# Attention loads issued one step ahead, two buffers for a head's keys and queries, attention steps dealt over fewer slices

## The chip, the cores and the metric

The kernel runs on one core of one Trainium2 chip. The metric is the device time of one execution in microseconds (us); the figure for a kernel is the median of its runs. PE is TensorE, DVE VectorE, ACT ScalarE, POOL GpSimd; SP is SyncE, whose queue issues the DMAs spoken of here.

## What is computed

The reference, cut to what matters. The inputs are q, k, v of shape (4, 8, 576, 64), a memory M_prev with its normaliser z_prev, beta, and the weights of two feed-forward layers with 512 model columns and 1536 hidden columns.

```python
# attention, per batch b and head h (S = 576, D = 64)
scores = where(causal, -1e9, q @ k.T / sqrt(D)); a = softmax(scores)
local = a @ v
q_p = where(q > 0, q, exp(q) - 1) + 1
mem_out = (q_p @ M_prev) / (q_p @ z_prev + 1e-6)
out = g * mem_out + (1 - g) * local              # g = sigmoid(beta)
# tokens: (4 * 576) x 512, heads side by side
# layer 0
xn = x / rms(x) * rms_g
x = (silu(xn @ w_gate) * (xn @ w_val)) @ w_out
# layer 1
x = (sigmoid(x @ w_gate2) * (x @ w_val2)) @ w_out2
```

## The kernel before

The 2304 tokens are worked in five groups: group -1 holds the first 128 tokens of all four batches (512 columns), groups 0 to 3 the other 448 tokens of one batch each. For a group, both feed-forward layers run in 12 slices of 128 hidden columns: a slice loads its weights (`weights`, `slot`), makes the gate and value products (L961), the gate (`gated`: tanh on ACT at L981, products on DVE at L983, L986 and L990, the two halves of h at L998/L999 or L1005/L1006) and, one slice later, 12 output products (`out_share`, L1027). In the trace group -1 stands from about 45 to 266 us, group 0 to 464, group 1 to 664, group 2 to 852, group 3 to 1009.

While PE works on group g, the attention of group g+1 is made beside it. It is cut into steps, put in a row by `att_steps`: for each head u `att_qk` (loads keys kd and queries qd, two DMAs each into the two halves of the partitions, casts them on ACT and takes the remainder on DVE, L210 to L231), `att_scores` (scores on PE at L253, copied to SBUF by ACT at L550, maxima, softmax), `att_av`, after every second head `att_mem` (loads ph, exp(q) at L629, L630, L631, products with the memory at L638) and `att_measure` (loads qm for the group after, sums of absolute values at L188); once per group `att_vmax` and `att_vsplit` (L150 to L174: values in two f16 parts).

The steps are dealt between the slices by the main loop (L1437 to L1522). `DUE` says how many slices before the end of a group the last step is dealt, `HOLD` how many slices pass before the first, and `AFTER` behind which slice's gate (counted back) a step's instructions may be issued; each is indexed by g+1. A scheduler then sets the order of every engine's queue, and each engine works its queue in that order. SP's queue holds the loads of the attention and those of the weights. A tile with `bufs=1` has a single buffer, so its next load waits until the last reader of the one before is done.

## Time and profile before

| | |
|---|---|
| median of 3 runs | 1013.91 us (1009.89 to 1014.56) |
| the profiled execution, its own time | 1016.42 us |
| its span | 1014.6 us, mean granted clock of PE 0.996 |
| PE busy | 999.3 us (98%) |
| DVE, ACT, POOL busy | 832.1 (82%), 654.7 (65%), 201.8 us (20%) |
| DMA | 243.74 MB, 240 GB/s on average |

The profile is of one execution. Busy time of PE counts matmuls, at whichever clock they ran. An idle time in brackets behind a row of the timeline is that of its engine just before the instruction, with what ended it; xN says that N instructions of one form stand in one row.

### The profile page before, as it was taken

Reading aid. Unit: us, or ns where it says so; the run is one execution under the profiler, and the core shown is the slowest. Engines: PE = TensorE matmul, PEld = TensorE weight load, DVE = VectorE, ACT = ScalarE, POOL = GpSimd, SP = SyncE. Lnnn points to the kernel's source line nnn. Section 1 sums busy time; section 2 is a strip of 40 time slices with the busy share of each in tenths; the row PEclk is TensorE's granted clock in tenths of the full one; section 3 lists DMA queues with packets and bytes.
Section 4 is the critical chain, followed back from the end, with each engine's and each line's share of the span. In section 5 each row is a group of like instructions: output and inputs, shape, how many; then the busy total and the mean of one; then the engine's idle time right before and its main releaser. Section 6 shows DMA issues by size and latency. Waiting matters only on the chain.

```text
span 1014.6 us, 19021 instructions
## 1 busy us (share of the span) xinstructions
PE 999.3 (98%) x6721; PEld 700.0 (69%) x6721; DVE 832.1 (82%) x1826; ACT 654.7 (65%) x1238; POOL 201.8 (20%) x339
## 2 busy tenths in 40 slices
PE   9999999999999999999999999999999999999998
PEld 6878887888666676666666765555567556876885
DVE  6989999997769998775998977757779776995883
ACT  7668887786678888674778676535456353543452
POOL 4203221141004233300424432002133100000000
PEclk9999999999999999999999999999999999999999
DMA  9599998986894676498779856995544256836521
GB/s 350 180 373 398 345 352 257 376 308 200 272 368 172 224 251 229 177 322 240 246 257 322 266 179 224 309 340 167 174 144 167 83 159 212 284 135 226 201 84 37
DMA packets 102561, 243.74 MB, mean 240 GB/s; under 512 B 25154, under 2 KB 37058, under 8 KB 102466
## 3 DMA queue, kind: packets, MB, share of 16 engines
q1 hardware_dynamic: 102322, 242.41, 69.8%
q8 instruction: 53, 0.87, 0.3%
q14 instruction: 42, 0.34, 0.1%
q10 hardware_dynamic: 144, 0.11, 0.0%
HBM read 187.43 MB, written 51.38 MB: 235 GB/s over the span
## 4 chain that ended last, share of the span: by engine, by line
PE 65%; DVE 14%; issue 9%; DMA 6%; ACT 5%; POOL 1%; SPq 0%; DVEq 0%; POOLq 0%; ACTq 0%
PE po L1027 20%; PE pg L961 16%; PE pv L961 15%; PE pw L1137 7%; PE ps L253 2%; DMA qd<-in_qT 1%; PE pm L638 1%; POOL sc L555 1%; DVE mx L572 1%; DMA raw<-in_w 1%; DMA wr<-kept 1%; PE pav L589 1%; PE pav L591 1%; PE pav L590 1%; DVE w L878 1%
## 5 line engine op out<-in xcount | busy, mean ns | idle before, releaser
L555 POOL TENSOR_SCALAR_AFFINE_SELECT sc<-sc 128x128 f32<-128x128 f32 (+1 forms) x128 | 73.0, 583 | 194.1 <-ACT sc L550 193.3
L1027 PE MATMUL po<-h,ws 128*128 128x448 f16 (+2 forms) x468 | 107.6, 375 | 0.0
L961 PEld LDWEIGHTS <-ws 128*128 128x128 f16 x552 | 53.5, 99 | 53.1 <-issue 4.9
L1027 PE MATMUL po<-h,wl 128*128 128x448 f16 (+2 forms) x372 | 86.8, 376 | 0.1
L961 PEld LDWEIGHTS <-wr 128*128 128x128 f16 x552 | 52.8, 98 | 49.2 <-issue 3.5
L1027 PE MATMUL po<-h,wr 128*128 128x448 f16 (+1 forms) x384 | 84.9, 364 | 0.2 <-ACT h L1005 0.2
L574 POOL PARTITION_ALL_REDUCE mb<-mx x32 | 61.3, 1915 | 70.9 <-DVE mx L572 62.1
L981 ACT ACTIVATE t<-pg,unit 128x448 f32<-128x448 f32 x70 | 43.8, 626 | 40.3 <-PE pg L961 40.1
L550 ACT COPY sc<-ps 128x512 f32<-128x512 f32 (+1 forms) x96 | 52.7, 562 | 18.6 <-PE ps L253 18.5
L1027 PEld LDWEIGHTS po<-h,ws 128*128 128x128 f32 x300 | 55.9, 188 | 9.4
L961 PEld LDWEIGHTS <-wl 128*128 128x128 f16 x360 | 34.7, 98 | 31.7 <-issue 1.3
L253 PE MATMUL ps<-qq,kk 128*128 128x64 f16 (+2 forms) x280 | 53.2, 295 | 0.0
L237 ACT ACTIVATE sc<-sc,qs 128x1472 f32<-128x1472 f32 x24 | 36.6, 1526 | 23.4 <-DVE sc L580 15.4
L990 DVE SCALAR_TENSOR_TENSOR t<-t,pv 128x448 f32<-128x448 f32 (+1 forms) x52 | 32.7, 629 | 18.6 <-PE pv L961 18.3
L1027 PEld LDWEIGHTS po<-h,wl 128*128 128x128 f32 x228 | 42.5, 188 | 8.0 <-ACT h L998 0.5
L1027 PE MATMUL po<-h,wrl 128*128 128x448 f16 (+1 forms) x192 | 44.0, 374 | 1.6 <-ACT h L1005 1.4
L983 DVE SCALAR_TENSOR_TENSOR t<-t,pg 128x448 f32<-128x448 f32 (+2 forms) x50 | 30.9, 618 | 15.4 <-ACT t L981 15.3
L872 ACT ACTIVATE top<-raw 128x512 f16<-128x512 bf16 x50 | 38.0, 784 | 5.6 <-DMA raw<-in_w 4.4
L998 ACT CAST h<-t 128x448 fp32r<-128x448 f32 (+1 forms) x46 | 27.0, 586 | 19.6 <-DVE t L986 14.4
L572 DVE TENSOR_TENSOR mx<-mx,sc 128x320 f32<-128x320 f32 (+2 forms) x96 | 34.5, 359 | 4.0 <-POOL sc L555 3.1
L1155 ACT COPY sn<-pw 128x224 f32<-128x224 f32 x54 | 18.2, 341 | 30.0 <-PE pw L1137 27.9
L878 DVE SCALAR_TENSOR_TENSOR w<-raw,top 128x512 int32<-128x512 int32 x48 | 35.3, 747 | 0.8 <-ACT top L872 0.6
(437 smaller groups left out, 2870.0 us busy)
## 6 DMA issues: line engine op xcount, KB each, us to landing
raw<-in_w SPq DMA_DIRECT2D x50, 511.8 KB, 6.4
kept<-w SPq DMA_DIRECT2D x48, 256.0 KB, 5.2
ws<-parts SPq DMA_DIRECT2D x24, 512.0 KB, 5.4
wr<-half SPq DMA_DIRECT2D x23, 512.0 KB, 4.1
rawl<-in_w SPq DMA_DIRECT2D x22, 511.8 KB, 6.5
wr<-parts SPq DMA_DIRECT2D x21, 512.0 KB, 5.6
ws<-half SPq DMA_DIRECT2D x21, 512.0 KB, 4.7
kd<-in_kT SPq DMA_DIRECT2D x64, 144.0 KB, 3.5
```

What stands on the lines that cost most here:

```text
L237: nc.scalar.activation(out=sc, in_=sc, func=AF.Exp, scale=both)
L253: nc.tensor.matmul(ps[:, c0:c0 + n], kk[:, k0:k0 + 128], r[:, q0 - 128:q0 - 128 + n], start=(i == 0), stop=(i == 1))
L550: nc.scalar.copy(out=sc[:, o:o + c], in_=ps[:, 0:c])
L555: nc.gpsimd.affine_select(out=d, in_=d, compare_op=ALU.is_ge, fill=NEG, base=SQ[kt] - T0[kt], pattern=[[1, n]], channel_multiplier=-1,)
L572: nc.vector.tensor_tensor(out=mx[:, q:448], in0=mx[:, q:448], in1=sc[:, d:d + 448 - q], op=ALU.max)
L574: nc.gpsimd.partition_all_reduce(mb[:, 0:448], mx[:, 0:448], channels=128, reduce_op=bass_isa.ReduceOp.max)
L872: nc.scalar.activation(out=top.bitcast(F16).rearrange("p (n t) -> p n t", t=2)[:, :, 1], in_=raw.bitcast(BF16)[:, :, 2], func=AF.Copy)
L878: nc.vector.scalar_tensor_tensor(out=dst.bitcast(I32), in0=raw.rearrange("p n t -> p (n t)").bitcast(I32).rearrange("p (n t) -> p n t", t= ...
L961: nc.tensor.matmul(ps[:, 0:n], w[:, a, k * 128:(k + 1) * 128], x[b][:, k, o:o + n], start=(i == 0), stop=(i == 3 * KD - 1))
L981: nc.scalar.activation(out=t, in_=pg[:, 0:n], func=AF.Tanh, scale=u[:, 0:1] if half else 0.5)
L1027: nc.tensor.matmul(po[d][:, 0:n], w[2][:, a, c], hh[:, b, 0:n], start=(first and i == 0), stop=(last and i == 2))
L1137: nc.tensor.matmul(regions[m][at], left(i, m, a, k), right(j, b, k), start=first and c == 0, stop=c == 5, skip_group_check=True,)
```

## The change

- `att_load` is new: it loads keys and queries of a head. kd and qd have two buffers each, and `att_qk` of head u issues the load of head u+1 (head 0 loads both).
- `mem_load` is new: ph of a pair of heads is loaded in an `att_av`, a step ahead of `att_mem`. `measure_load` is new: qm is loaded in `att_mem`, a step ahead of `att_measure`.
- The product with the memory goes into the tile of exp(q), where it had a tile mt of its own. qd, q2 and ph are 448 columns wide; tri stands in the ring w of the weights; the tiles sn of the last group follow kd's and qd's two buffers.
- `DUE` of group 0 goes from 6 to 8: the steps that make group 1's attention are dealt over 14 slices and no longer 16. `AFTER` of group 0 goes from 1 to 2.

```diff
@@ -36,10 +36,10 @@
 NSHARE = (2, 1)
 
 ONE = (1, 12)
-DUE = (3, 6, 6, 5, 8)
+DUE = (3, 8, 6, 5, 8)
 HOLD = (1, 2, 1, 1, 1)
 BACK = (3, 3)
-AFTER = (3, 1, 3, 3)
+AFTER = (3, 2, 3, 3)
 
 HALVED = 1
 
@@ -95,7 +95,7 @@
 
     ident = const.tile([128, 128], F32, name="ident")
     make_identity(nc, ident)
-    tri = const.tile([128, 128], F32, name="tri")
+    tri = wp.tile([128, 512], F32, tag="w", bufs=4, name="tri")[:, 0:128]
     nc.gpsimd.memset(tri, 0.0)
     nc.gpsimd.affine_select(
         out=tri, in_=tri, compare_op=ALU.is_ge, fill=NEG, base=0, pattern=[[1, 128]], channel_multiplier=-1
@@ -127,7 +127,7 @@
 
     q2_ring = []
     for i in range(2):
-        t = const.tile([128, S], F32R, name=f"q2_{i}")
+        t = const.tile([128, S - 128], F32R, name=f"q2_{i}")
         nc.vector.memset(t[64:128].bitcast(F32), 0.0)
         q2_ring.append(t)
     vh1 = const.tile([128, 5, H, 65], F16, name="vh1")
@@ -178,13 +178,18 @@
 
     qring = [0]
 
+    def measure_load(g, u):
+        st["qm", g, u] = []
+        for src, c0 in ((kT, 0), (qT, 128)):
+            t = ap_.tile([128, S], F32, tag="qm", bufs=2, name="qm")[:, c0:S]
+            nc.sync.dma_start(out=t, in_=src[g, 2 * u:2 * u + 2, :, c0:S].rearrange("h d s -> (h d) s"))
+            st["qm", g, u].append(t)
+
     def att_measure(g, u):
 
         if u == 0:
             st["sums", g] = ap_.tile([128, NP, 2], F32, tag="qsum", bufs=1, name="qsum")
-        for i, (src, c0) in enumerate(((kT, 0), (qT, 128))):
-            t = ap_.tile([128, S], F32, tag="qm", bufs=2, name="qm")[:, c0:S]
-            nc.sync.dma_start(out=t, in_=src[g, 2 * u:2 * u + 2, :, c0:S].rearrange("h d s -> (h d) s"))
+        for i, t in enumerate(st.pop(("qm", g, u))):
             nc.scalar.activation(out=t, in_=t, func=AF.Abs, accum_out=st["sums", g][:, u, i:i + 1])
 
     def att_units(g):
@@ -202,18 +207,25 @@
         )
         st["qs", g] = qs
 
-    def att_qk(g, u):
-        kd = ap_.tile([128, S], F32, tag="kd", bufs=1, name="kd")
-        qd = ap_.tile([128, S], F32, tag="qd", bufs=1, name="qd")[:, 128:S]
+    def att_load(g, u):
+        kd = ap_.tile([128, S], F32, tag="kd", bufs=2, name="kd")
+        qd = ap_.tile([128, S - 128], F32, tag="qd", bufs=2, name="qd")
         for src, dst, c0 in ((kT, kd, 0), (qT, qd, 128)):
             for j in range(2):
                 nc.sync.dma_start(out=dst[64 * j:64 * j + 64], in_=src[g, u, :, c0:S])
+        st["load", g, u] = kd, qd
+
+    def att_qk(g, u):
+        if u == 0:
+            att_load(g, u)
+        if u + 1 < H:
+            att_load(g, u + 1)
+        kd, qd = st.pop(("load", g, u))
         if g < HALVED:
             q2 = q2_ring[qring[0] % 2]
             qring[0] += 1
             kk = ap_.tile([128, S], F32R, tag="kk", bufs=2, name="kk")
             qq = ap_.tile([128, S], F32R, tag="qq", bufs=2, name="qq")[:, 128:S]
-            q2 = q2[:, 128:S]
             nc.scalar.activation(out=kk, in_=kd, func=AF.Copy)
             nc.scalar.activation(out=qq, in_=qd, func=AF.Copy)
             for out, d, hi, r in ((kk, kd, kk, slice(64, 128)), (q2, qd, qq, slice(0, 64))):
@@ -601,6 +613,8 @@
         nc.vector.tensor_tensor(out=out, in0=ps[:, :, 0:64], in1=r.to_broadcast([128, n, 64]), op=ALU.mult)
 
     def att_av(g, h):
+        if h % 2 == (0 if g >= HALVED else 1):
+            mem_load(g, h // 2)
         pt = st.pop(("pt", g, h))
         s = st[g]
         ps = late["ps"].tile([128, 4, 65], F32, tag="pa", name="pav")
@@ -619,13 +633,18 @@
         nc.vector.reciprocal(out=r, in_=r)
         nc.vector.tensor_tensor(out=out, in0=ps[:, :, :, 0:64], in1=r.to_broadcast([128, 2, 2, 64]), op=ALU.mult)
 
+    def mem_load(g, u):
+        ph = st["ph", g, u] = ap_.tile([128, S - 128], F32, tag="ph", bufs=1, name="ph")
+        nc.sync.dma_start(out=ph, in_=qT[g, 2 * u:2 * u + 2, :, 128:S].rearrange("h d s -> (h d) s"))
+
     def att_mem(g, u):
 
         x = st[g]["x"]
         n = 448
-        ph = ap_.tile([128, 512], F32, tag="ph", bufs=1, name="ph")
+        ph = st.pop(("ph", g, u))
+        if HALVED <= g + 1 < B:
+            measure_load(g + 1, u)
         e = ap_.tile([128, 512], F32, tag="xn", bufs=2, name="phe")
-        nc.sync.dma_start(out=ph[:, 0:n], in_=qT[g, 2 * u:2 * u + 2, :, 128:S].rearrange("h d s -> (h d) s"))
         nc.scalar.activation(out=e[:, 0:n], in_=ph[:, 0:n], func=AF.Exp)
         nc.vector.tensor_scalar(out=e[:, 0:n], in0=e[:, 0:n], scalar1=1.0, scalar2=None, op0=ALU.min)
         nc.vector.scalar_tensor_tensor(
@@ -643,7 +662,7 @@
                     stop=True,
                 )
             gt = igate[:, None, 2 * u:2 * u + 2, None].to_broadcast([128, 2, 2, 1])
-            m = ap_.tile([128, 2, 2, 64], F32, tag="mt", bufs=2, name="mt")
+            m = e[:, 256 * i:256 * i + 256].rearrange("p (t h d) -> p t h d", t=2, h=2)
             mem_out(ps, gt, m)
             xs = x[:, 2 * i:2 * i + 2, u * 128:(u + 1) * 128]
             nc.vector.tensor_tensor(out=xs, in0=xs, in1=m.rearrange("p t h d -> p t (h d)"), op=ALU.add)
@@ -1147,7 +1166,7 @@
         cs = []
         for m, tag in ((0, "kk"), (1, "qq")):
             cs.append([ap_.tile([128, S], F32, tag=tag, bufs=2, name="cw")[:, 0:2 * n] for _ in range(2)])
-        one = [ap_.tile([128, S], F32, tag=t, bufs=1, name="sn") for t in ("kd", "qd")]
+        one = [ap_.tile([128, w], F32, tag=t, bufs=2, name="sn") for t, w in (("kd", S), ("qd", S - 128))]
         three = [ap_.tile([128, 512], F32, tag=t, bufs=1, name="sn") for t in ("mx", "mb")]
         snaps = [[one[m][:, 0:n], one[m][:, n:2 * n], three[m][:, 0:n]] for m in range(2)]
 
```

The instructions of an engine are the same in number; lines of the changed program stand up to 19 further down (L981 is L1000, L629 is L648, L1027 is L1046). Three places of the order follow. In the names, t and h are the tiles of the gate, pg and po the sums of the gate and output products, ws, wl, wr, wrl weights, x the values.

First ACT near the end of group 1's steps in group 0 (425 us in the trace). Before:

```order
L1005 ACTIVATE h<-t,unit_124 128x448
L246 CAST pt<-sc 128x1472
L830 ACTIVATE ws,sums<-ws 128x512 x2
L629 ACTIVATE phe<-ph 128x448
L550 COPY sc<-ps_5353 128x448
L981 ACTIVATE t<-pg,unit_124 128x448
L550 COPY sc<-ps_5360 128x512
L1005 ACTIVATE h<-t,unit_124 128x448
```

and with the change:

```order
L1024 ACTIVATE h<-t,unit_124 128x448
L849 ACTIVATE ws,sums<-ws 128x512 x2
L562 COPY sc<-ps_5193 128x512
L1000 ACTIVATE t<-pg,unit_124 128x448
L865 COPY unit_123<-inv 128x2
L866 ACTIVATE unit_124<-inv 128x2
L855 ACTIVATE ws<-ws,s_5837 128x512 x2
L648 ACTIVATE phe<-ph 128x448
L562 COPY sc<-ps_5203 128x448
L1024 ACTIVATE h<-t,unit_124 128x448
```

The exponential (phe) stood ahead of the gate's L981; it now stands behind the gate's L1000, two copies of units and two weight scalings. A copy of scores (sc) has moved behind the sums of ws.

Second DVE in the first heads of group 1 (300 to 306 us in the trace), from one slice's h to the next slice's t. Before:

```order
L999 TENSOR_TENSOR h<-t,h 128x448
L150 TENSOR_REDUCE am_3797<-x 128x1 x5
L715 TENSOR_SCALAR pw<-wtop 128x2
L230 SCALAR_TENSOR_TENSOR kk<-kd,qs,kk 64x576
L230 SCALAR_TENSOR_TENSOR qq<-qd,qs,qq 64x448
L153 TENSOR_REDUCE am<-am_3797 128x1
L569 TENSOR_TENSOR mx<-sc 128x448
L717 TENSOR_SCALAR inv<-pw 128x2
L983 SCALAR_TENSOR_TENSOR t<-t,pg 128x448
```

and with the change:

```order
L1018 TENSOR_TENSOR h<-t,h 128x448
L856 SCALAR_TENSOR_TENSOR ws<-wrl,s_3976,ws 128x512 x2
L734 TENSOR_SCALAR pw<-wtop 128x2
L736 TENSOR_SCALAR inv<-pw 128x2
L740 RECIPROCAL s_4153<-inv 128x2
L174 SCALAR_TENSOR_TENSOR vl<-x,sv,vh_119 128x512 x2
L581 TENSOR_TENSOR mx<-sc 128x448
L174 SCALAR_TENSOR_TENSOR vl<-x,sv,vh_119 128x512 x3
L1002 SCALAR_TENSOR_TENSOR t<-t,pg 128x448
```

The five residuals of the values (vl) stood behind this t and now stand ahead of it; the five maxima (am) and a head's kk and qq that stood here are dealt with elsewhere, the maxima further up.

Third PE in group -1 (147 to 151 us in the trace), scores of one head among the output products. Before:

```order
L1027 MATMUL po<-h,wl 128x512 x4
L253 MATMUL ps_1798<-qq,kk 128x448
L253 MATMUL ps_1798<-q_0_115,kk 128x448
L1027 MATMUL po<-h,wl 128x512 x8
L253 MATMUL ps_1805<-qq,kk 128x320
L253 MATMUL ps_1805<-q_0_115,kk 128x320
L253 MATMUL ps_1805<-qq,kk 128x192
L253 MATMUL ps_1805<-q_0_115,kk 128x192
L961 MATMUL pg<-xc,wl 128x512
```

and with the change:

```order
L1046 MATMUL po<-h,wl 128x512 x4
L265 MATMUL ps_1802<-qq,kk 128x448
L265 MATMUL ps_1802<-q_0_115,kk 128x448
L265 MATMUL ps_1809<-qq,kk 128x320
L265 MATMUL ps_1809<-q_0_115,kk 128x320
L265 MATMUL ps_1809<-qq,kk 128x192
L265 MATMUL ps_1809<-q_0_115,kk 128x192
L1046 MATMUL po<-h,wl 128x512 x8
L980 MATMUL pg<-xc,wl 128x512
```

The second part of the scores stood behind eight of the output products and now stands ahead of them.

## Rows read from the trace of the kernel before

**Rows 1.** The page, parts 1 and 2: busy time of the engines, PE's granted clock.

```profile
PE 999.3 (98%) x6721; PEld 700.0 (69%) x6721; DVE 832.1 (82%) x1826; ACT 654.7 (65%) x1238; POOL 201.8 (20%) x339
...
PEclk9999999999999999999999999999999999999999
```

**Rows 2.** Waits of PE: engine, line, released by; us in total, times, longest us.

```profile
PE pg L961 <- DMA ws<-half: 1.8, 1, 1.8
PE pg L961 <- DVE t L983: 1.6, 3, 0.7
PE po L1027 <- ACT h L1005: 1.6, 2, 1.4
```

**Rows 3.** Stretches (start:end, length; busy of PE, PEld, DVE, ACT, POOL, PEclk, DMA share, GB/s).

```profile
150.00:190.00 40.00, 39.31 (x211) 31.37 (x211) 39.63 (x75) 33.10 (x55) 5.50 (x8) 1.00 0.87 292
300.00:340.00 40.00, 39.28 (x270) 24.86 (x269) 39.11 (x85) 35.06 (x73) 13.87 (x26) 1.00 0.57 194
```

**Rows 4.** The two 10 us stretches with PE's long waits, same columns.

```profile
420.00:430.00 10.00, 8.36 (x69) 6.55 (x67) 7.49 (x26) 6.89 (x17) 4.26 (x8) 0.85 0.02 6
580.00:590.00 10.00, 7.94 (x33) 4.01 (x32) 6.66 (x21) 8.21 (x16) 5.14 (x7) 0.83 0.43 141
```

**Rows 5.** Timeline at 425 us on ACT, DVE, PE; last, 12 matmuls elsewhere (start, us, engine, instruction).

```profile
420.49 0.58 ACT L629 ACTIVATE phe<-ph 128x448 f32<-128x448 f32 x1 [0.58 <-DMA ph<-in_qT]
420.98 0.52 ACT L550 COPY sc<-ps 128x448 f32<-128x448 f32 x1
...
424.81 0.67 ACT L1005 ACTIVATE h<-t,unit 128x448 fp32r<-128x448 f32 x1 [2.31 <-DVE t L990]
...
421.10 0.39 DVE L630 TENSOR_SCALAR phe<-phe 128x448 f32<-128x448 f32 x1 [2.06 <-ACT phe L629]
...
424.16 0.62 DVE L990 SCALAR_TENSOR_TENSOR t<-t,pv 128x448 f32<-128x448 f32 x1
...
425.53 0.67 PE L1027 MATMUL po<-h,wrl 128*128 128x448 f32 x2 [1.37 <-ACT h L1005]
426.48 3.71 PE L1027 MATMUL po<-h,wrl 128*128 128x448 f32 x10 [0.28 <-DVE h L1006]
...
563.74 2.68 PE L1027 MATMUL po<-h,wl 128*128 128x448 f32 x12
```

**Rows 6.** Timeline at 583 us: SP's issue, PE.

```profile
578.47 0.58 SPq L903 DMA_DIRECT2D ws<-half  x1
...
583.43 4.13 PE L961 MATMUL pg<-hb,ws 128*128 128x448 f16 x12 [1.84 <-DMA ws<-half]
```

**Rows 7.** Waits of SP: line, released by; us in total, times, longest us.

```profile
SPq L210 <- DVE kk L230: 33.6, 15, 5.0
```

**Rows 8.** Groups of ACT: busy us, mean ns of one, idle us just before.

```profile
L227 ACT ACTIVATE kk<-kd,qs 128x576 f16<-128x576 f32 x24 | 18.6, 773 | 0.0
...
L629 ACT ACTIVATE phe<-ph 128x448 f32<-128x448 f32 x16 | 9.2, 574 | 3.2 <-DMA ph<-in_qT 3.2
...
L217 ACT ACTIVATE kk<-kd 128x576 fp32r<-128x576 f32 x8 | 5.5, 684 | 1.7 <-DMA kd<-in_kT 1.7
```

**Rows 9.** Timeline at 305 to 320 us: PE, then DVE.

```profile
309.09 2.43 PE L961 MATMUL pg<-ha,ws 128*128 128x448 f16 x12
...
317.75 2.43 PE L961 MATMUL pg<-ha,ws 128*128 128x448 f16 x12 [0.69 <-DVE t L983]
...
305.64 0.61 DVE L983 SCALAR_TENSOR_TENSOR t<-t,pg 128x448 f32<-128x448 f32 x1
306.17 0.14 DVE L158 TENSOR_SCALAR ex<-amx 128x1 int32<-128x1 int32 x1
...
312.57 2.71 DVE L174 SCALAR_TENSOR_TENSOR vl<-x,sv,vh 128x512 f16<-128x512 f32 x4
```

**Rows 10.** Timeline at 150 us: PE, then ACT.

```profile
148.45 2.02 PE L1027 MATMUL po<-h,wl 128*128 128x512 f32 x8
...
148.84 0.52 ACT L550 COPY sc<-ps 128x448 f32<-128x448 f32 x1
```

## The prediction

> **What bounds the kernel now.** I read the page first. TensorE (PE) is busy 999.3 us of a span of 1014.6, VectorE (DVE) 82%, ScalarE (ACT) 65%; PE's granted clock is at nine tenths of full or more in every slice [rows 1]. So PE bounds the kernel, and all that a new order can win is PE's idle time, 1014.6 - 999.3 = 15.3 us, and what a low clock costs. Second, PE's list of waits: the longest single ones are 1.8 us for a load of ws and 1.4 us for ACT's h; three for DVE's t hold 1.6 us in all, 0.7 at most [rows 2]. Third, the stretches: DVE is the engine to watch, at 39.63 of 40 us in group -1 and at 39.11 of 40 early in group 0, where PE misses 0.72 us [rows 3]; the two 10 us stretches with PE's long waits show a granted clock of 0.85 and 0.83, between the full and the half level [rows 4]. Last, the timelines at these two places:
>
> - Stall A, 425 us: the output product L1027 waits 1.37 us for ACT's h; its 12 matmuls, among them 0.28 us more of waiting, then take from 425.53 to 426.48 + 3.71 = 430.19, 4.66 us, against 2.68 us for 12 of the same form at 563.74 [rows 5]. Price: 1.37 + 4.66 - 2.68 = 3.35, some 3.4 us.
> - Stall B, 583 us: the gate product waits 1.84 us for ws, and its 12 matmuls take 4.13 us against 2.43 for 12 at 309 us [rows 6, 9]. Price: 1.84 + 1.70 = 3.5 us.
>
> **The change part by part.**
>
> *Keys and queries in two buffers, loaded a head ahead.* No DMA is added. Only an engine that waited for these loads can gain: ACT idled 0.0 us ahead of the 24 casts L227 and 1.7 us ahead of the 8 copies L217 (the first group's attention) [rows 8], and PE's longest waits have none on kd or qd [rows 2]. What hides the loads is work that ACT has queued ahead of the casts. SP issues all loads in order, and waits 33.6 us in 15 places for DVE's subtraction L230 before it can load kd or qd [rows 7]. The change does not take that away: the load of head u+1 is issued at step u, into the buffer of head u-1, whose last reader is the subtraction of head u-1, the same that SP waited for. The second buffer gives data one step earlier, but frees nothing queued behind kd on SP. At stall B that is the load of ws, issued at 578.47 [rows 6], and SP's order there is the same in the change. I take 0 us; bounds -1.7 (all of L217's idle) and +1.84 (one more weight load as late as ws at 583 us, because kd or qd stands ahead of it).
>
> The Trainium skill says under "DMA: Bandwidth & Descriptors", Rules for kernel authors, that a DMA should be issued early and waited for late. By that rule this part would win ACT's waits on kd, and the sum would be up to 1.7 us lower. The same page, section "Anatomy of one DMA — SWDGE (gpsimd) path", says that a semaphore wait happens on the issuing sequencer before dispatch, which speaks against the part; the trace agrees, with 33.6 us on SP, and by it the sum stays.
>
> *ph loaded ahead of its step, qm likewise.* ACT idled 3.2 us in all ahead of the 16 exponentials L629 [rows 8]. One of these reaches PE, and it is stall A: ACT came free at 420.49 - 0.58 = 419.91 and waited 0.58 us for ph, with a copy and the gate's L981 queued behind it. DVE waited 2.06 us for that exponential and then ran L630, L631 and maxima ahead of L990, from 421.10 to 424.16, 3.06 us; ACT's h followed at 424.81 and PE at 425.53 [rows 5]. The first excerpt shows the exponential behind the gate's activation, so the gate is earlier by 420.98 - 419.91 = 1.07 us. On DVE, L990 stands ahead of L630 in the change, so the 3.06 us leave the chain too, less two products of weights that come ahead instead (some 1.4 us by L174, 2.71 for four of the same width [rows 9]). 1.07 + 3.06 - 1.4 = 2.7 us is more than the 1.37 us that PE waited. I take all of stall A, -3.4 us. Bounds: -3.4, and 0, since ACT's sums of ws, which wait for their own load, still stand ahead of the gate, and h may be late again. qm: loaded a step before use, and no long wait of PE is behind it [rows 2]: 0 us.
>
> *mt dropped, tri in the ring w, q2 of 448 columns, sn in two buffers.* The same instructions on other tiles. The product with the memory makes e live longer, but e has two buffers and its exponential runs 16 times in 1014 us; tri is read before the slices begin: 0 us.
>
> *Steps of group 1 dealt over 14 of group 0's slices instead of 16, and issued one slice sooner.* The work is the same; it comes earlier, when DVE is full. The second excerpt shows the sharpest place of group 0: the five residuals L174 (2.71 us for four, 3.4 for five) and, further up, the scale's five small steps L158 to L165 (some 0.14 each, 0.7) now stand ahead of the gate's t (L983), 4.1 us more work before it. That t ended at 305.64 + 0.61 = 306.25, and PE's next gate product, which needs the bank that t frees, started at 309.09: 2.84 us of slack [rows 9]. That makes a new wait of 4.1 - 2.84 = 1.3 us. Against it, the wait of 0.69 us at 317.75 goes [rows 9], since the residuals that stood ahead of it are done. In group -1 the third excerpt has the second part of a head's scores ahead of eight output products. These began at 148.45, so the scores are now wanted then; the bank that they need is freed by ACT's copy, which ended at 148.84 + 0.52 = 149.36 [rows 10], and ACT has one more cast of a query ahead of it (some 0.5 us, by the copy of the same width): a new wait of 149.36 - 148.45 + 0.5 = 1.4 us. Both are upper ends, since a wait delays PE and so eases the next. I take half of each, +0.7 and +0.7. Bounds: 0, and the full waits with a half clock behind each, below. Groups 1 and 2 keep their order on PE, ACT, DVE and POOL, 0 us. The slices from 430 us on that lose their steps gain nothing: PE had no long wait there.
>
> **Sum.** -3.4 (A) - 0.7 (317 us) + 0.7 + 0.7 - 0.4 (one of the two other waits on DVE's t, (1.6 - 0.7)/2 [rows 2]) = -3.1. The profiled execution took 1016.42 us (span 1014.6), 2.5 above the median of the runs shown; 1016.42 - 3.1 = 1013.3, and, by the same 2.5, 1010.8 for a median. I say **1011 us**.
>
> **Rivals.**
>
> - *Faster: both drops of the clock go.* If the steps and loads that come sooner let SP reach ws at 583 us by 1.84 us earlier, stall B goes with A and the waits on DVE's t: -3.4 - 3.5 - 1.6 = -8.5, 1013.9 - 8.5 = 1005.4. For it: a shift of under 2 us is enough, and SP waits for DVE there. Against it: SP's order and DVE's order in group 1 are the same as before. Chance 0.17.
> - *Slower: the work dealt earlier makes DVE late.* Place: the gate's t at 306 us and the scores at 148 us. Price: 1.3 and 1.4 us waited, and behind each a stretch at half clock like those behind the waits of 1.37 and 1.84, worth 2.0 and 1.7 [rows 5, 6, 9]: 6.4 in all. It decides from the point where a new wait is as long as 1.37 us; behind the 0.69 at 317.75 the next 12 matmuls took 2.43, no loss [rows 9]. With stall A gone, 1013.9 + 6.4 - 3.4 = 1016.9; with stall A only moved, 1020.3. DVE at 39.11 and 39.63 of 40 us [rows 3] speaks for it; that each wait lets DVE catch up speaks against. Chance 0.18.
> - *No effect.* The loads were hidden, SP waits for the same subtraction, and stall A comes back as another late h. 1014 us. Chance 0.20.
>
> **How the numbers follow.** The forecast has the other 0.45, from 1007 to 1014. A measurement of this kernel tells about 0.5% (5 us) from no change: its three runs lie from 1009.9 to 1014.6. Faster by over that, below 1008.8: the faster rival's 0.17 and 0.11 of the forecast's, 0.28. Slower, over 1019: 0.12 of the slower rival and 0.03 of the case of no effect, 0.15. The rest, 0.57, is within it. The range runs from 1004, just under the faster rival, to 1019, between the slower one's two values; some 0.07 is left out below and 0.13 above.
>
> **What would show it.** Right: no wait of PE on ACT's h near 420 us and a clock of 1.00 there; the drop near 583 us still there, with PE on ws; SP's wait for DVE's subtraction still some 30 us; a wait of PE on DVE's t near 305 to 310 us. Wrong: the second drop gone, or a new one near 150 or 310 us; SP's wait for the subtraction halved, which would mean that the second buffer does free the queue; or a stage other than groups -1 and 0 that changed its length by over 2 us.

## The result and the profile after

The changed kernel took 1018.67 us (median of 6 runs, 1018.26 to 1022.8) against 1013.6 us of the kernel before in the same series: ratio 1.0064, 95% interval 1.0047 to 1.0081. In a second series it was 1019.03 against 1014.53 us, 1.0051 (1.0031 to 1.0071). So it is slower by 0.5 to 0.6%, some 5 to 6 us. The forecast was 1011 us and faster; the range (1004 to 1019) holds the result, the direction was wrong. In the later series the kernel before had medians from 1012.65 to 1014.53 us.

The page of the changed kernel's profile (span 1019.7 us), which answers to [rows 1]:

```profile
PE 998.2 (98%) x6721; PEld 698.0 (68%) x6721; DVE 831.1 (82%) x1826; ACT 656.1 (64%) x1238; POOL 204.9 (20%) x339
...
PEclk9999999999999999999999999999999999999999
```

PE is busy 998.2 us, 1.1 less than before, in a span 5.1 us longer. The whole loss is idle time of PE. Its list of waits (engine, line, what it waited for; us in total, times, longest) answers to [rows 2]:

```profile
PE pg L980 <- DVE t L1002: 4.3, 3, 3.2
PE pg L980 <- DMA ws<-half: 2.0, 1, 2.0
PE pg L980 <- DMA ha<-x: 2.0, 2, 1.3
PE ps L265 <- ACT sc L562: 1.4, 2, 0.8
...
PE pv L980 <- DVE t L1007: 1.1, 1, 1.1
```

Stall A, 1.4 us for ACT's h [rows 2], is gone. Stall B (ws) stands as before. New are 3.2 us in one wait for DVE's t L1002 (before: 0.7 at most), 1.3 for ha, which holds the tokens of group 1, 1.1 for DVE's t L1007, and 0.8 for the scores' copy. Two stretches of the same profile (columns as in [rows 3]), the first one answering to [rows 4]:

```profile
420.00:430.00 10.00, 10.00 (x58) 6.49 (x57) 8.45 (x18) 8.91 (x21) 1.81 (x5) 1.00 0.70 246
310.00:320.00 10.00, 6.24 (x26) 2.69 (x25) 9.63 (x17) 9.77 (x21) 3.64 (x8) 0.83 0.54 189
```

At 420 us, where before had lost 1.64 of 10 us at a granted clock of 0.85, PE is full at 1.00. Instead the stretch at 310 us, where before had no long wait [rows 9], loses 3.76 us at 0.83.

One profile is one execution, so I took three of before's order (the one shown, a repeat, and before_eph, a kernel with the same order) and three of the change's (the one shown, a repeat, and own_step_phqm, a kernel with the same order). PE's idle time by stretch, which is the length of the stretch less the time PE was busy in it, us:

| from, to (us) | before's order | change's order | mean difference |
|---|---|---|---|
| 0, 45 | 3.3, 3.7, 3.3 | 3.3, 3.3, 3.9 | +0.1 |
| 45, 262 (group -1) | 0.7, 0.7, 0.7 | 2.8, 3.1, 2.9 | +2.3 |
| 262, 300 | 0.6, 0.6, 0.6 | 0.7, 0.8, 0.7 | +0.1 |
| 300, 345 | 0.7, 0.9, 0.9 | 3.8, 3.2, 1.9 | +2.1 |
| 345, 400 | 0.4, 0.5, 0.4 | 0.8, 0.5, 1.9 | +0.7 |
| 400, 460 (stall A) | 1.6, 0.3, 1.5 | 0.0, 0.1, 0.0 | -1.1 |
| 460, 478 (tokens of group 1) | 0.0, 0.0, 0.0 | 1.3, 1.4, 1.7 | +1.5 |
| 478, 600 (stall B in it) | 3.0, 3.3, 3.2 | 3.4, 3.9, 2.4 | +0.1 |
| 600, end | 5.0, 5.0, 5.1 | 5.3, 5.4, 5.4 | +0.3 |
| idle in all | 15.3, 14.9, 15.7 | 21.5, 21.7, 20.7 | +6.0 |
| PE busy | 999.3, 994.4, 995.7 | 998.2, 995.7, 995.3 | -0.1 |
| span | 1014.6, 1009.3, 1011.4 | 1019.7, 1017.4, 1016.0 | +5.9 |

The idle time accounts for the whole difference of the spans, 5.9 us, and that is about the measured 5 to 6. The rest of the document asks what makes the new waits in group -1, at 310 us and at 464 to 477 us.

### The profile page after: what moved, and what is told of

The parts are those of the page before. It is cut to its first block, busy times and chain, and to the rows that moved or that the text cites. A ratio compares the mean times of both kernels' runs of the same rounds, so it can differ in the third digit from the quotient of the medians.

```text
span 1019.7 us, 18970 instructions
## 1 busy us (share of the span) xinstructions
PE 998.2 (98%) x6721; PEld 698.0 (68%) x6721; DVE 831.1 (82%) x1826; ACT 656.1 (64%) x1238; POOL 204.9 (20%) x339
## 4 chain that ended last, share of the span: by engine, by line
PE 75%; DMA 11%; DVE 8%; ACT 3%; issue 1%; POOL 1%; SPq 1%; ACTq 0%; POOLq 0%; DVEq 0%
PE po L1046 22%; PE pg L980 20%; PE pv L980 19%; PE pw L1156 7%; PE ps L265 3%; DMA kept<-w 2%; DMA raw<-in_w 2%; PE pm L657 1%; DMA ws<-kept 1%; PE pav L601 1%; PE pav L603 1%; PE pav L602 1%; DMA kd<-in_kT 1%; DMA rawl<-in_w 1%; DMA qk<-in_qk 1%
## 5 line engine op out<-in xcount | busy, mean ns | idle before, releaser
L1046 PE MATMUL po<-h,ws 128*128 128x448 f16 (+2 forms) x468 | 108.3, 376 | 0.3 <-ACT h L1017 0.3
L567 POOL TENSOR_SCALAR_AFFINE_SELECT sc<-sc 128x128 f32<-128x128 f32 (+1 forms) x128 | 68.8, 551 | 190.6 <-ACT sc L562 189.4
L980 PEld LDWEIGHTS <-ws 128*128 128x128 f16 x552 | 53.5, 99 | 57.6 <-issue 10.6
L1046 PE MATMUL po<-h,wl 128*128 128x448 f16 (+2 forms) x372 | 87.7, 376 | 0.3
L1046 PE MATMUL po<-h,wr 128*128 128x448 f16 (+1 forms) x384 | 86.2, 366 | 0.1
L586 POOL PARTITION_ALL_REDUCE mb<-mx x32 | 65.1, 2033 | 54.4 <-DVE mx L584 45.8
L1000 ACT ACTIVATE t<-pg,unit 128x448 f32<-128x448 f32 x70 | 43.9, 627 | 45.9 <-PE pg L980 45.6
L1046 PEld LDWEIGHTS po<-h,ws 128*128 128x128 f32 x300 | 55.6, 188 | 9.9 <-ACT h L1017 0.7
L1046 PEld LDWEIGHTS po<-h,wl 128*128 128x128 f32 x228 | 42.1, 188 | 8.1 <-DVE hb L1231 0.9
L1002 DVE SCALAR_TENSOR_TENSOR t<-t,pg 128x448 f32<-128x448 f32 (+2 forms) x50 | 30.9, 617 | 18.5 <-ACT t L1000 18.2
L1046 PE MATMUL po<-h,wrl 128*128 128x448 f16 (+1 forms) x192 | 43.4, 367 | 0.0
L587 DVE TENSOR_TENSOR sc<-sc,mb 128x896 f32<-128x896 f32 x32 | 34.8, 1087 | 3.8 <-POOL mb L586 3.8
```

What stands on the lines that cost most here:

```text
L567: nc.gpsimd.affine_select(out=d, in_=d, compare_op=ALU.is_ge, fill=NEG, base=SQ[kt] - T0[kt], pattern=[[1, n]], channel_multiplier=-1,)
L586: nc.gpsimd.partition_all_reduce(mb[:, 0:448], mx[:, 0:448], channels=128, reduce_op=bass_isa.ReduceOp.max)
L587: nc.vector.tensor_tensor(out=two, in0=two, in1=mb[:, None, 0:448].to_broadcast([128, 2, 448]), op=ALU.subtract)
L980: nc.tensor.matmul(ps[:, 0:n], w[:, a, k * 128:(k + 1) * 128], x[b][:, k, o:o + n], start=(i == 0), stop=(i == 3 * KD - 1))
L1000: nc.scalar.activation(out=t, in_=pg[:, 0:n], func=AF.Tanh, scale=u[:, 0:1] if half else 0.5)
L1046: nc.tensor.matmul(po[d][:, 0:n], w[2][:, a, c], hh[:, b, 0:n], start=(first and i == 0), stop=(last and i == 2))
```

## The experiments

### One part at a time

Four kernels on one chip; before 1012.71 us there. The theory was that the dealing alone costs, the rival that the loads do.

*loads_only*: the change with the dealing of before.

```diff
-DUE = (3, 8, 6, 5, 8)
-AFTER = (3, 2, 3, 3)
+DUE = (3, 6, 6, 5, 8)
+AFTER = (3, 1, 3, 3)
```

> The changed kernel with the old dealing (DUE 6, AFTER 1 for group 0). Theory 1 (the dealing costs: it takes a head's loads of keys and queries ahead of weight loads on SP, and the residuals ahead of the gate's t): no wait of PE on DVE's t above 0.9 us at 305 to 320 us, ACT does not wait over 1 us for the weight load wrl<-kept there, stall A near 425 us still gone (the exponential stands behind the gate here too), the 1.4 us that group -1 lost stay; 1010 to 1013 us. Theory 2 (the early loads cost by themselves): the wait of 3 us near 314 us is there, 1016 us or more.

*deal_only*: the kernel before with the dealing of the change (the same lines the other way round).

> The kernel before with the new dealing alone (DUE 8, AFTER 2 for group 0), kd and qd in one buffer and loaded in their own step. Theory 1 (dealing): PE waits 2.5 to 3.5 us for DVE's t near 310 to 316 us with a drop of the clock behind it, SP issues wrl<-kept near 290 us behind a kd load that waited some 3 us for the subtraction, ACT waits 2 to 3 us for that weight load; stall A gone; 1014 to 1018 us. Theory 2 (early loads): no such wait, 1009 to 1012 us.

*own_step_kq*: the change, with two buffers for a head's keys and queries but each loaded in its own step.

```diff
 def att_qk(g, u):
-    if u == 0:
-        att_load(g, u)
-    if u + 1 < H:
-        att_load(g, u + 1)
+    att_load(g, u)
```

> The changed kernel with kd and qd loaded in their own step again (two buffers kept). Theory 1 (dealing): the wait near 314 us stays at 2.5 to 3.5 us, since in SP's order the next head's load stands at the same place and only its name differs; here it finds a free buffer, so if SP's wait in front of it is what makes the weights late, the wait of PE shrinks to 1 to 2 us. Time 1015 to 1018. Theory 2 (early loads): the wait is gone, at most 1013 us.

*own_step_phqm*: the change, with `mem_load` and `measure_load` called in the steps that use the data.

> The changed kernel with ph and qm loaded in their own steps again. If stall A went because the exponential stands behind the gate (an effect of the order that the dealing gave), it stays away here and the time is that of the changed kernel, 1017 to 1020 us. If it went because ph came a step sooner, a wait of PE on ACT's h of over 1 us is back near 430 us, with 3 us more.

| kernel | median us | ratio to before (95%) |
|---|---|---|
| loads_only | 1022.36 | 1.0089 (1.0072 to 1.0107) |
| deal_only | 1015.24 | 1.0022 (1.0011 to 1.0034) |
| own_step_kq | 1018.22 | 1.0045 (1.0029 to 1.0061) |
| own_step_phqm | 1019.13 | 1.0060 (1.0039 to 1.0080) |

Both theories fall as pure ones: the loads alone cost more than the whole change, and the dealing alone less than half of it. The parts don't add. Nor did the waits come as the expectations had them: the wait for DVE's t that the dealing was to lengthen to 2.5 to 3.5 us was 1.4 us in deal_only and 0.7 in own_step_kq, and loads_only had 1.4 us. Calling `mem_load` and `measure_load` in their own steps gives the change's time: every engine has the same order there, SP too. Stall A stayed away, so the order took it away and not an earlier ph.

### The dealing taken apart, and the buffers

*due_only* and *after_only*: before with DUE 8 alone, and with AFTER 2 alone. *one_buf*: the change with single buffers (kd, qd and the last group's sn) and a head's loads in their own steps, whose order is that of deal_only; the diff shows the buffers of kd and qd. *before_again*: before, unchanged, for a second profile.

```diff
-        kd = ap_.tile([128, S], F32, tag="kd", bufs=2, name="kd")
-        qd = ap_.tile([128, S - 128], F32, tag="qd", bufs=2, name="qd")
+        kd = ap_.tile([128, S], F32, tag="kd", bufs=1, name="kd")
+        qd = ap_.tile([128, S - 128], F32, tag="qd", bufs=1, name="qd")
```

> The kernel before with DUE 8 alone (AFTER stays 1). In its order the first heads of group 1 stand as before (residuals behind the gate's t, kd behind the weight loads on SP) and the exponential near 425 us stands behind the gate. Theory A (the wait at 310 us comes from AFTER): at 300 to 345 us PE's waits as before, 0.9 us; stall A gone; a wait for the tokens of group 1 near 464 us of 1 to 2 us, as in all kernels that lost stall A; time 1010 to 1013. Theory B (from DUE): waits of 2 to 3 us at 300 to 345 us and 1015 us.

> The kernel before with AFTER 2 alone (DUE stays 6). In its order the residuals stand ahead of the gate's t and kd ahead of two weight loads on SP, as in the changed kernel. Theory A: waits of PE of 2 to 3 us at 300 to 345 us, time 1014 to 1016. Theory B: 0.9 us there, at most 1013.

> The changed kernel with a single buffer for kd and qd, loaded in their own step; the product in e's tile, ph and qm ahead, q2, tri and the dealing as in the change. Every engine's order is that of the dealing alone (deal_only, 1015.2). If the second buffers cost the rest (through the order that they change in group -1, in group 0 and in the last group), this gives 1014 to 1016; if the longer life of e or the early ph do, 1017 to 1019 as own_step_kq.

> The kernel before, unchanged, for a second trace. If the drops of the clock behind the waits near 425 and 583 us come and go from execution to execution, while the waits of 1.4 and 1.8 us stay, then the 3.4 us that the forecast booked for stall A were 1.4 of waiting and 2.0 of chance; here a span of 1009 to 1011 us with the granted clock near 1.00 in one or both places. If the drops belong to the waits, the span is 1014 to 1015 us again with both drops.

due_only: 1025.23 us, 1.0129 (1.0107 to 1.0152). after_only: 1025.51 us, 1.0119 (1.0099 to 1.0139). Each half of the dealing costs some 12 us, both together 2.5. Both runs missed every forecast, 1010 to 1016 us; neither theory had the idle time of PE at 345 to 400 us, 4.7 and 4.6 us. one_buf: 1016.95 us, 1.0038 (1.0017 to 1.0059), not told apart from deal_only. So a price can't be given for an edit by itself: each edit deals every queue anew, and the price is that of the order that comes out.

The repeat of before took 1011.07 us, and its timeline (start, us, engine, instruction, idle time before it) shows what stall A had been. ACT, then PE:

```profile
417.40 0.58 ACT L629 ACTIVATE phe<-ph 128x448 f32<-128x448 f32 x1 [0.58 <-DMA ph<-in_qT]
...
421.72 0.67 ACT L1005 ACTIVATE h<-t,unit 128x448 fp32r<-128x448 f32 x1 [2.31 <-DVE t L990]
...
422.39 1.06 PE L1027 MATMUL po<-h,wr 128*128 128x448 f32 x4
423.29 2.59 PE L1027 MATMUL po<-h,wrl 128*128 128x448 f32 x12
```

The same chain stands here as in [rows 5], with the same 0.58 us for ph and the same 2.31 us for DVE's t, and the 12 products with wrl don't wait at all and take 2.59 us: in this execution h is ready as PE comes to it. The third execution (before_eph, below) waited 0.95 us there, and its granted clock stayed at 1.00. The 3.35 us of stall A were the dearest of three executions.

### Parts that move no instruction, and another queue

*before_eph*: before with ph loaded a step ahead and the memory products in e's tile. *before_kdpool* and *after_kdpool*: before and the change with the loads of keys and queries on POOL's queue.

```diff
-                nc.sync.dma_start(out=dst[64 * j:64 * j + 64], in_=src[g, u, :, c0:S])
+                nc.gpsimd.dma_start(out=dst[64 * j:64 * j + 64], in_=src[g, u, :, c0:S])
```

> The kernel before with two parts of the change that leave every engine's order as it was: ph loaded one step ahead, and the memory products in exp(q)'s tile. Theory (these parts cost and win nothing; stall A at 425 us was one execution's chance): median as before within 0.25% (1010.5 to 1015.5 us), ACT's wait for ph near 417 us gone. Rival (stall A is ph's late load and stands in every execution, as the prediction had it): about 3 us less, a median near 1010 us. Rival (these parts bring part of the change's loss): 1 us or more above before with an interval that excludes 1.

> The kernel before with the loads of keys and queries issued from POOL's queue and no longer from SP's. Theory (SP's queue, standing behind a buffer that DVE has not freed, is what makes weight loads late): SP's waits for the subtraction vanish, so the wait of PE for ws near 583 us (about 2 us in every trace) goes, and the median falls by 1 to 4 us. Rival (the scheduler deals all engines' orders anew, and DVE and DMA are full where it matters): ws still late somewhere, and the median is 2 to 12 us above before, as with the other new orders.

> The change with the loads of keys and queries issued from POOL's queue. Theory (part of the change's loss at 300 to 345 us comes from weight loads that stand behind a head's keys on SP): the waits of PE at 300 to 345 us, 5.5 us in the profile of the change, fall to about 2 (as before), and the median is 2 to 4 us below the change's 1018.7. Rival (the residuals dealt ahead of the gate on DVE are the cause by themselves): a wait of over 1.3 us at about 310 us stays, and the median stays at 1017 or above.

before_eph: 1013.16 us, 1.0006 (0.9994 to 1.0018): nothing, as the theory had it; but it was wrong that ACT's wait for ph would go. The groups of ACT (busy us, mean ns | idle before), first of before_eph, then of the change:

```profile
L634 ACT ACTIVATE phe<-ph 128x448 f32<-128x448 f32 x16 | 9.2, 573 | 3.0 <-DMA ph<-in_qT 3.0
```

```profile
L239 ACT ACTIVATE kk<-kd,qs 128x576 f16<-128x576 f32 x24 | 18.6, 776 | 0.0
...
L648 ACT ACTIVATE phe<-ph 128x448 f32<-128x448 f32 x16 | 9.2, 573 | 3.4 <-DMA ph<-in_qT 3.3
...
L229 ACT ACTIVATE kk<-kd 128x576 fp32r<-128x576 f32 x8 | 5.5, 684 | 3.2 <-DMA kd<-in_kT 3.2
```

The exponential waits 3.0 and 3.3 us for ph where before had 3.2 [rows 8]. In before_eph the load is written one step sooner in the program, but SP's order is before's row for row, so it is issued where it was. And the first group's copies of keys, which an earlier load was to help, wait 3.2 us in the change where they waited 1.7.

before_kdpool: 1032.55 us, 1.0190 (1.0173 to 1.0208); after_kdpool: 1032.95 us, 1.0206 (1.0187 to 1.0224). With the loads on POOL's queue both kernels are far slower, with every engine's order changed (in before_kdpool PE waited 6.4 us at once for ACT's wrl; the longest wait of before is 1.8 [rows 2]). SP no longer waits for the subtraction, but POOL does, in before_kdpool 36.6 and 32.9 us in its two forms, with its own work queued behind. Two places came out as the theory of SP's queue had them: PE waited only 0.5 us for ws near 583 us in before_kdpool, and idled only 1.0 us between 300 and 345 us in after_kdpool. Since the whole order differs, neither shows the theory.

### Early issue against second buffers

*own_due6*: own_step_kq with the dealing of before, so second buffers without early issue and without the new dealing. *kq_from_g1*: the change, with early issue only where `g >= HALVED`, so not beside group -1. *after_again*: the change once more. Before 1014.53 us there.

```diff
-        if u == 0:
+        if u == 0 or g < HALVED:
             att_load(g, u)
-        if u + 1 < H:
+        if u + 1 < H and g >= HALVED:
             att_load(g, u + 1)
```

> The change with the dealing of before (6, 1) and with a head's keys and queries in two buffers but loaded in the head's own step. The early issue alone is what this lacks against the run with the loads alone (1022.4 us). Theory (issuing early in group -1, where the DMA engines are full, is the price: 2.1 us of waits at 99, 117 and 150 us and late tokens after it): those waits gone, median 1014 to 1017. Rival (the second buffer, which lets the scheduler put the casts and loads elsewhere, is the price): median 1019 or more, and 0.5 us or less of new waits in group -1.

> The change whole, but that the early issue of keys and queries begins with the attention of the group with 16-bit casts; the first group's attention, made beside group -1, loads in its own steps. Every engine's order is that of the run with own-step loads, but for two rows of SP. Theory (the early issue costs 2 us in group -1 and nothing later): no wait over 0.5 us at 99, 117 and 150 us but the 0.4 and 1.0 of before, and a median as with own-step loads, 1018.2, within 1 us. Rival (the early issue in the later groups is what costs or wins): more than 2 us from that.

> The change unchanged, a second profile beside the others. If its waits are the order's, the list by stage repeats that of the first profile: 2.1 us of waits in group -1 that before has not, 3 to 5.5 us at 300 to 345 us (before 1.6 to 1.7), over 1 us for the tokens at 464 to 477 us; if they are one execution's chance, they stand elsewhere. Median 1018 to 1020.

own_due6: 1021.76 us, 1.0080 (1.0059 to 1.0100), and no new wait in group -1: the rival is right. With the old dealing it is an order that costs, and not the early issue; that the second buffers bring this order is argued from before_eph, where ph and the tile of e cost nothing. kq_from_g1: 1018.89 us, 1.0051 (1.0031 to 1.0071), after_again 1019.03 us, the same ratio. PE's waits from 45 to 260 us, first of after_again, then of kq_from_g1:

```profile
PE pv L980 <- DVE t L1007: 1.4, 1, 1.4
PE ps L265 <- ACT sc L562: 0.8, 1, 0.8
PE pg L980 <- DVE t L1002: 0.7, 1, 0.7
```

```profile
PE ps L265 <- ACT sc L562: 0.3, 1, 0.3
PE pg L980 <- ACT t L1000: 0.2, 1, 0.2
```

So the early issue makes the waits in group -1: PE idles 2.7 to 3.1 us there in all four profiles that have it, 0.6 to 0.8 in all others with the loads on SP. kq_from_g1 differs from the change in group -1 alone, but there in the order of every engine, so the loads that go sooner and the order that they bring are not parted. And taking these waits out did not make a median that can be told from the change's. What eats the 2.3 us is open: kq_from_g1's one profile is of its fastest run, 1016.75 us.

### Where the last attention step stands

The wait for group 1's tokens (PE on ha at 464 to 477 us) was 0 in before's order, 1.3 to 1.8 in the change, deal_only and the other kernels with its dealing and the loads on SP, 2.9 in the two kernels with the loads on POOL, and 3.1 to 4.1 in loads_only, own_due6, due_only and after_only. Group 1's tokens are done only after its last attention step: the last product with the memory, DVE's sums, the norm, the transposes. The distance on PE from that product to the first gate product of group 1 is read from PE's timeline, here of the repeat of before, of after_again, and of own_due6:

```profile
438.70 0.61 PE L638 MATMUL pm<-mzt,ph 128*128 128x130 f32 x4
...
461.00 2.45 PE L961 MATMUL pg<-ha,ws 128*128 128x448 f16 x12
```

```profile
447.55 0.69 PE L657 MATMUL pm<-mzt,ph 128*128 128x130 f32 x4
...
468.36 2.43 PE L980 MATMUL pg<-ha,ws 128*128 128x448 f16 x12 [1.39 <-DMA ha<-x]
```

```profile
454.30 0.61 PE L654 MATMUL pm<-mzt,ph 128*128 128x130 f32 x4
...
471.90 3.65 PE L977 MATMUL pg<-ha,ws 128*128 128x448 f16 x12 [4.06 <-DMA ha<-x]
```

Before, PE came to the gate 461.00 - 438.70 = 22.3 us after the product (22.3 in all three profiles) and waited for nothing. In the change it came 468.36 - 1.39 - 447.55 = 19.4 us after it, the same 19.4 in deal_only, own_step_kq and own_step_phqm. In own_due6 it was 471.90 - 4.06 - 454.30 = 13.5. DUE was raised to deal the steps sooner, and the last one came out nearer to the end. If the distance makes the wait, an order with the product further ahead has none. *due10_after2*, *due10_after1* and *due9_after1* are before with the values of DUE and AFTER in their names for group 0, whose orders have it so; the first one's diff:

```diff
-DUE = (3, 6, 6, 5, 8)
-AFTER = (3, 1, 3, 3)
+DUE = (3, 10, 6, 5, 8)
+AFTER = (3, 2, 3, 3)
```

> The kernel before with DUE of group 0 at 10 and AFTER at 2: steps dealt over 12 slices. In the order of PE the last product of group 1's attention with the memory now stands further ahead of the group's first slice than in before; in the change it stands nearer to it, although DUE went up. Theory (that distance sets the wait for group 1's tokens at 464 to 477 us: none in before, 1.4 in the change, 3.1 to 4.1 where the distance is least): no wait for the tokens; the five residuals ahead of the gate on DVE still make one of 1 to 3 us near 310 us; median 1013 to 1017. Rival (the tokens come late because DVE is late all through group 0): a wait of over 1 us for the tokens again, and a median of 1016 or more.

> The same with AFTER left at 1. Theory of the distance: no wait for the tokens. Two of the residuals stand ahead of the gate on DVE, as in before, so 1 us or less at 310 us; median 1012 to 1017, and if the work dealt sooner makes no other wait it equals or beats before. Rival (whatever is dealt sooner comes back as other waits in 300 to 400 us): 1018 or more.

> The same with DUE at 9 and AFTER at 1, one slice more to deal over. Theory of the distance: no wait for the tokens, median within 2 us of the run with 10 and 1. Rival as there.

The distances were 33.5, 27.8 and 25.7 us, and there was no wait for the tokens in any of the three. due10_after2, the same two events:

```profile
440.22 0.69 PE L638 MATMUL pm<-mzt,ph 128*128 128x130 f32 x4
...
473.68 2.45 PE L961 MATMUL pg<-ha,ws 128*128 128x448 f16 x12
```

So the distance sets that wait, to within a few us. In the 13 profiles with a wait the tokens were ready 17.6 to 21.2 us after the product began, at distances of 13.5 to 19.4 us; in the six with 22.3 us or more there was none. The times were 1024.01 us, 1.0102 (1.0082 to 1.0122); 1024.13, 1.0104 (1.0079 to 1.0128); and 1020.19, 1.0071 (1.0053 to 1.0088): as slow as the rivals had it, without the wait for the tokens by which the first rival explained it, and 9 with 1 was not within 2 us of 10 with 1. What dealing sooner saved at 470 us it lost at 300 to 400 us: PE idled 10.1, 6.4 and 4.9 us there, against 1.4 in the repeat of before. In due10_after2 PE's waits from 300 to 400 us are led by the same gate:

```profile
PE pg L961 <- DVE t L983: 6.7, 2, 5.1
PE pg L961 <- ACT t L981: 1.8, 1, 1.8
```

### The place at 310 us

It is read from the traces. The timeline of the change's first profile on SP, ACT, DVE and PE:

```profile
287.82 1.17 SPq L215 DMA_DIRECT2D kd<-in_kT  x2
289.09 1.18 SPq L215 DMA_DIRECT2D qd<-in_qT  x2
...
293.32 1.00 SPq L934 DMA_DIRECT2D ws<-kept  x1
...
306.19 0.63 ACT L849 ACTIVATE ws<-ws 128x512 f16<-128x512 f32 x1 [2.56 <-DMA ws<-kept]
...
307.56 1.41 DVE L856 SCALAR_TENSOR_TENSOR ws<-wrl,s,ws 128x512 f16<-128x512 f32 x2 [3.23 <-ACT ws L855]
...
309.88 1.41 DVE L174 SCALAR_TENSOR_TENSOR vl<-x,sv,vh 128x512 f16<-128x512 f32 x2
...
312.02 2.07 DVE L174 SCALAR_TENSOR_TENSOR vl<-x,sv,vh 128x512 f16<-128x512 f32 x3
314.01 0.61 DVE L1002 SCALAR_TENSOR_TENSOR t<-t,pg 128x448 f32<-128x448 f32 x1
...
314.68 4.11 PE L980 MATMUL pg<-ha,ws 128*128 128x448 f16 x12 [3.15 <-DVE t L1002]
```

and the repeat of before, SP and DVE:

```profile
291.18 0.43 SPq L915 DMA_DIRECT2D ws<-kept  x1
293.18 1.92 SPq L210 DMA_DIRECT2D kd<-in_kT  x2
...
305.06 0.61 DVE L983 SCALAR_TENSOR_TENSOR t<-t,pg 128x448 f32<-128x448 f32 x1
...
311.25 0.74 DVE L174 SCALAR_TENSOR_TENSOR vl<-x,sv,vh 128x512 f16<-128x512 f32 x1
311.99 2.71 DVE L174 SCALAR_TENSOR_TENSOR vl<-x,sv,vh 128x512 f16<-128x512 f32 x4
```

Before, the five residuals (L174) stand behind the gate's t and wait for nothing that matters; in the change they stand ahead of it, and so do two products of weights (L856), which wait for ACT, as ACT waits for the load ws<-kept. Before, the loads of kd and qd stand behind ws<-kept on SP; in the change they stand ahead of it, and SP waited 3.0 us to issue them (3.6 us in after_again). So two things lie ahead of t: more work on DVE, and weights that land late. deal_only has the same order on DVE and SP at this place, and SP waited 3.2 us at its kd too, but its weights came almost in time. Its SP, ACT, DVE and PE:

```profile
286.86 1.17 SPq L210 DMA_DIRECT2D kd<-in_kT  x2
...
292.37 0.50 SPq L915 DMA_DIRECT2D ws<-kept  x1
...
301.94 0.63 ACT L830 ACTIVATE ws<-ws 128x512 f16<-128x512 f32 x1 [0.19 <-DMA ws<-kept]
...
303.31 1.42 DVE L837 SCALAR_TENSOR_TENSOR ws<-wrl,s,ws 128x512 f16<-128x512 f32 x2 [0.87 <-ACT ws L836]
...
310.42 2.43 PE L961 MATMUL pg<-ha,ws 128*128 128x448 f16 x12 [1.38 <-DVE t L983]
```

Eight profiles have this order on DVE at this place. DVE's wait for ACT's weights and PE's wait for t, and the time from the issue of ws<-kept to its landing, us:

| kernel | ws<-kept, issue to landing | DVE for ACT | PE for t |
|---|---|---|---|
| own_step_phqm | 8.6 | 0.58 | 1.40 |
| deal_only | 9.5 | 0.87 | 1.38 |
| own_step_kq | 9.5 | 0.87 | 0.72 |
| kq_from_g1 | 10.0 | 1.31 | 2.30 |
| after_again | 10.4 | 1.70 | 2.64 |
| after_only | 10.6 | 2.60 | 2.10 |
| one_buf | 11.7 | 3.14 | 3.16 |
| the change | 12.8 | 3.23 | 3.15 |

So with the weights almost in time the order on DVE makes PE wait 0.7 to 1.4 us, and where they land late it waits up to 3.2. SP's stop at kd is not enough for that: deal_only and own_step_kq have it (3.2 and 2.9 us), and ACT waited 0.2 us for these weights. The landing differs between executions of one order (9.5 us in deal_only, 11.7 in one_buf). In before's three profiles it took 7.9 to 8.8 us; whether kd ahead of the weights is what makes it longer is not shown.

## Why the prediction was wrong

- **Stall A, -3.4 us: right that it goes, wrong in size.** The step "I take all of stall A, -3.4 us" fails. The stall is gone in the change's order and in deal_only's. In three executions of before's order PE idled 1.6, 0.3 and 1.5 us from 400 to 460 us, and the 12 products took 4.66 us, against 2.68 elsewhere, in one of them alone. So the gain was 1.1 us of idle time on average, and the 2.0 us of clock once in three; it was not 3.4 each time. The text had the warning in hand: it says that the profiled execution was 2.5 us above the median, and subtracted a stall of that execution from the median all the same.
- **ph loaded early: the mechanism was not there.** In before_eph and the change, ACT waits for ph as long as before. I took the place in the program for the place on SP; SP's order would have told. What put the exponential behind the gate's activation was the new order: deal_only, with no early ph, has it too, and so has own_due6, with the dealing of before.
- **Keys and queries in two buffers, 0 us with bounds -1.7 and +1.84: wrong.** "What hides the loads" was right, no cast of the 24 waits. But with the second buffers the scheduler puts everything else in another order. With the old dealing and no early issue the ratio was 1.0080 (1.0059 to 1.0100). With the new dealing it can't be told from none: own_step_kq 1.0045 (1.0029 to 1.0061) against one_buf 1.0038 (1.0017 to 1.0059). SP's wait for DVE's subtraction was not freed, as the text said it would not be; it rose from 33.6 [rows 7] to 40.8 us (the change's waits of SP):

```profile
SPq L215 <- DVE kk L242: 40.8, 16, 7.5
```

  It stands in 16 places instead of 15. The longest grew from 5.0 to 7.5 us, and that came with the dealing: deal_only has 7.7 at single buffers. The Trainium skill, "DMA: Bandwidth & Descriptors", Rules for kernel authors, says to issue a DMA early and to wait for it late. That won nothing here: the first group's copies waited 2.5 to 3.3 us in the four profiles with the early issue, and 1.0 to 2.5 in the others with the loads on SP. The same page, "Anatomy of one DMA — SWDGE (gpsimd) path", says that a semaphore wait happens on the issuing sequencer before dispatch. The trace agrees: SP stood 3.0 us at kd at 287 us, with the loads of weights behind it.

- **150 us, +0.7: about right in size, given to the wrong part.** The wait of 0.8 us for the scores' copy is there. But the order of the third excerpt came with the early loads and not with the dealing, under which the text had it: deal_only and kq_from_g1 keep the eight output products ahead of the second part of the scores. The early loads and their order made two more waits in group -1 that the forecast did not have, 1.1 and 1.4 us for t L1007 near 99 us and 0.7 for t L1002 near 118. The full DMA engines and DVE (39.63 of 40 us [rows 3]) were read, and not held against loads that come earlier.
- **306 to 309 us, +0.7: the right place, the wrong size.** The forecast had no loss from 300 to 345 us in sum, +0.7 for the new wait and -0.7 for the one at 317 us; PE's idle time there rose by 2.1 us. The step "Both are upper ends ... I take half of each" fails: the full 1.3 was not an upper end. PE waited 1.4 us where the weights came almost in time (deal_only), and 3.15 where they landed late. The 4.1 us of work put ahead of t left out the two products of weights (1.41 us) that the second excerpt shows there, and with them DVE's wait for ACT and ACT's for the load.
- **"The slices from 430 us on that lose their steps gain nothing": wrong.** The last step came nearer to the group's end, by 22.3 - 19.4 = 2.9 us of PE's time, and 1.3 to 1.7 us of waiting for the tokens came with it. The sum had nothing for this. This was in PE's order and I looked only at the places where steps moved forward.
- **sn in two buffers, 0 us: wrong by 0.3 us.** A wait of PE of 0.27 us at 888 to 903 us stands in every profile with the second buffers of kd, qd and sn, and not in before, deal_only and one_buf.
- **Stall B stays:** right, 2.0 us of waiting (1.6 and 1.8 in the two others of the change's order).
- **The slower rival** named DVE's lateness at 306 and 148 us, and 1016.9 or 1020.3 us; the time lay between, and PE lost time at both its places. That its time fits is luck in part. It had 3.7 us for the clock behind the two waits, and PE's mean busy time did not rise; in their place stand the tokens' 1.5 us and the waits at 99 and 118 us, which it did not name. It had 0.18 because the waits were thought to pay for each other; in the table the new waits add up to the whole loss.

## What to carry over

A stall seen in one profile is a price only when it comes again: take a second profile, or at least see whether the profiled execution is slower than the median, before it is booked as a gain. A wait behind a load has a size that differs too: here the same order gave 1.4 us with the weights in time and 3.2 without. When a scheduler or a table of numbers deals the work, read the whole order that comes out, on every queue: what a moved step itself waits for, and above all where the last step goes that the next stage waits for. An edit written earlier in the program may move nothing, and one that only adds a buffer may move everything.

## What was not expected of the hardware

The loss of clock behind a wait comes in one execution and not in another. At 314 us the change's first profile waited 3.15 us, and the 12 matmuls behind it took 4.11 us at a granted clock of 0.83 in that stretch. In the second profile, after 2.64 us:

```profile
314.57 2.43 PE L980 MATMUL pg<-ha,ws 128*128 128x448 f16 x12 [2.64 <-DVE t L1002]
```

The 12 took 2.43 us, at 1.00. At stall A the clock was 0.85 in the profile of before and 1.00 in before_eph, behind 0.95 us. The loss at 314 us is 4.11 - 2.43 = 1.7 us, and the two profiled executions took 1021.5 and 1019.2 us. The slower rival's mark, a loss from a wait of 1.37 us on, does not hold as a rule. Of the 53 waits of PE of 1.3 to 3.2 us from 45 to 1000 us in the 19 profiles, 24 had a mean granted clock of 0.50 to 0.68 in the 4 us behind them, which is the half level for all or most of that time, and 29 had 1.00; the longest with no loss was 3.16 us (one_buf, 312 us). Such a loss belongs in a range and not in a sum.
